# A window-attention and Fourier-mix kernel: constants loaded in another step, start masks and sink halves in other steps and on another engine, transposes in another order

## The chip, the cores and the metric

The kernel runs on one core of one Trainium2 chip. The core has five engines that work side by side, each through its own queue of instructions in order: TensorE (PE, matrix products, with its weight loads shown as PEld), VectorE (DVE), ScalarE (ACT), GpSimd (POOL) and SyncE (SP), which issues loads and stores. POOL can issue loads too, into a queue of its own. Sixteen DMA engines carry out what the queues hold. Engines wait for one another by semaphores.

The metric is device time in microseconds (us) of one launch. The kernel before ran three times: 782.7, 784.17 and 782.69 us, median 782.7 us.

## The reference

```python
B, H, S, D = 4, 8, 768, 64; n_sink, window = 4, 128; d_model = 512
scores = (q @ k^T) / sqrt(D)
keep   = (key < n_sink) | (0 <= query - key < window)
a      = softmax(where(keep, scores, -1e9))
x      = (a @ v), heads side by side          # B x 768 x 512
u      = x + real(fft(fft(x, axis=1), axis=2))
un     = (u - mean(u)) / sqrt(var(u) + 1e-6)
out    = u + relu(un @ w_ch1) @ w_ch2         # 512 -> 2048 -> 512
```

So there are three things in a row: attention with four sink keys and a window of 128 keys, a two-dimensional Fourier transform of which the real part is added, and a feed-forward block. The input `window` is read at run time, so the masks are made on the chip.

## The kernel before

**Attention in steps.** The 24 blocks of 128 queries (4 batches of 6) are taken one after the other, in the batch order 0, 2, 1, 3. Each block g is worked on in four steps s = 4g + k, one for each pair of heads. A step's work is spread over later steps as a software pipeline. `STEP_LAG` says how many steps later each part runs: scores on PE and the merge and masked reduction on DVE in the step itself (`merge`, `soft1`), the exponentials on ACT two steps later (`expo`), the transposes `pt` of the probabilities on PE three later (`trans_p`), ACT's copy `pta` four later, POOL's two selections five later (`newer_p`, `older_p`), the products `xt` with the values seven later (`av`). `BLOCK_AT` gives the same for work done once per block, counted from step 4g: `floor` (POOL adds 1e-9 to the sums), `inverse` (DVE's reciprocal of them, L743), `trans_sink` (PE's transpose `pk` of the sink probabilities), `turn_x` (PE's `x`, which turns the block's result and adds the sink part) and `store_x` (DVE scales by the reciprocal).

**Order within a step.** `SCHEDULE` has two phases, before step 36 and from 36 on, and in each phase a list for every engine and each k: the order in which the engine's pieces are issued in that step. The names "A", "V", "G", "T" in a list stand for events of that engine: one-off pieces that `at(step, engine, fn)` has put there, such as the parts of the Fourier transform on PE ("T"). The scores are issued two steps at a time, ahead of the T list, into two PSUM buffers. Up to step 97 (`CUT`) this hand-made order holds; behind it an automatic scheduler orders what is left.

**Loads.** SP loads a block's queries and keys two blocks ahead (`q`, `ring`, or both in `ld` for a batch's first block), the values `ldv`, and a batch's sink values `vt`. `ring` is a ring of eight key blocks. A score product whose two key blocks wrap around the end of the ring waits for every load into the ring that was issued before it; that is so in step 28 (block 7).

**The start.** ACT turns the sink values into a high half `vs` (`sink_hi`, L682) and DVE writes the low half into the other partitions (`sink_lo`, L686); for the first batch this happens in step `SINK0_AT`. DVE makes the masks: mask 0 ahead of step 0, then `other_masks` in step 4 (L885 to L895: the two `older` masks, which say where the window's older block is to be merged, and the sink columns and window columns of masks 1 to 3), and `last_mask` in step 6.

**Fourier mix.** Its constants `cst` (3348 KB) and `cst_row` (322 KB) are loaded once, by POOL, in `load_constants` (L292 to L296), which also clears `sph` and `zr`. It is called in step 4, ahead of that step's POOL events. As the blocks of a batch are done, DVE and POOL fold them, and PE runs stage 1 in five pieces (za, za, zr, zb, zb), each in one or two parts. After each piece ACT copies a high half (`z_hi`) and DVE forms the low half (`z_lo`) in the step that follows the piece's last part (L487). Stage 1's pieces take turns in PSUM with the transposes; in steps 81 to 97 they have one bank.

**Feed-forward.** High and low halves again, products of 128x512 on PE (`h`, `o`). They begin beside the attention and fill PE alone from about 280 us to the end.

## Time and profile before

| what | before |
|---|---|
| runs | 782.7, 784.17, 782.69 us |
| the profiled execution | 786.08 us |
| its span, first to last instruction | 784.1 us |
| mean granted PE clock | 0.991 |
| busy: PE, DVE, ACT, POOL | 755.7, 453.5, 237.1, 185.1 us |
| bytes moved | 57.67 MB |

The profile page is one execution. Its second part cuts the span into 40 equal slices and gives each engine's busy share in tenths. A row of the timeline has the start, the duration, the engine, the line of the code, what is written and read, a count where equal instructions are put together, and in brackets the idle time of the engine before it and the instruction that ended that. A row of the windows has, for a stretch of the span, the busy time of each engine, then the granted clock of PE, the mean busy share of the sixteen DMA engines and what they moved in GB/s. A row of the waits has the engine and line, what it waited for, the total, how often, and the longest. All stand at the prediction.

### The profile page before, as it was taken

To read this page: it belongs to the slowest core of one execution; us is meant where nothing else is said; L and a number is where in the kernel's file an instruction comes from. 1 tells how busy PE (TensorE), PEld (TensorE's weight loads), DVE (VectorE), ACT (ScalarE), POOL (GpSimd) and SP (SyncE) were. 2 spreads that over 40 slices of the span, in tenths; PEclk is the share of its full clock that TensorE was granted. 3 is DMA by queue.
4 is the path that set the end of the run, shared out by engine and by line. 5 is a ranking of instruction groups with operands and counts; after the bars stand their busy time and mean duration, and the time that the engine had idled before them with its cause. 6 is when DMAs were issued, how large, how long until landed. Compare 5 with 4: busy or idle time off the path is not lost.

```text
span 784.1 us, 11917 instructions
## 1 busy us (share of the span) xinstructions
PE 755.7 (96%) x4379; PEld 616.8 (79%) x4379; DVE 453.5 (58%) x1330; ACT 237.1 (30%) x704; POOL 185.1 (24%) x307
## 2 busy tenths in 40 slices
PE   7999998989998999999999999999999999999996
PEld 5676876867777878899888888888888888888895
DVE  6878587999999489561456424661456424611211
ACT  4887765766523123221111101111111111110110
POOL 2567477477654255100000000000000000000000
PEclk9999999999999899999999999999999999999998
DMA  9863535434215266110100002000200001000100
GB/s 283 268 177 105 151 83 177 127 112 145 86 50 166 92 196 208 66 59 1 54 0 1 1 18 89 1 0 1 81 0 1 2 1 54 1 0 1 54 1 31
DMA packets 41810, 57.67 MB, mean 74 GB/s; under 512 B 2796, under 2 KB 27500, under 8 KB 41360
## 3 DMA queue, kind: packets, MB, share of 16 engines
q1 hardware_dynamic: 41456, 53.07, 21.6%
q0 software_dynamic: 288, 3.76, 1.3%
q8 instruction: 36, 0.59, 0.3%
q14 instruction: 30, 0.25, 0.1%
HBM read 47.37 MB, written 9.45 MB: 72 GB/s over the span
## 4 chain that ended last, share of the span: by engine, by line
PE 80%; DVE 9%; POOL 4%; issue 3%; ACT 2%; DMA 2%; SPq 1%; POOLq 0%; DVEq 0%; ACTq 0%
PE o L1126 33%; PE h L620 33%; PE s L703 3%; PE xt L793 3%; PE pt L755 2%; PE za L395 1%; DVE cv L592 1%; DVE cv L593 1%; DVE sm L721 1%; PE zb L395 1%; ACT pta L762 1%; ACT sm L727 1%; DMA vt<-in_v_sink_dram 1%; POOL ptl L771 1%; DVE s L709 1%
## 5 line engine op out<-in xcount | busy, mean ns | idle before, releaser
L1126 PE MATMUL o<-w,h 128*128 128x512 f32 x876 | 218.6, 397 | 0.0
L1119 DVE SCALAR_TENSOR_TENSOR h<-h,h 128x512 fp32r<-128x512 f32 (+1 forms) x107 | 65.4, 611 | 250.5 <-ACT h L1114 250.3
L1126 PEld LDWEIGHTS o<-w,h 128*128 128x128 f32 x876 | 164.5, 190 | 36.0
L1114 ACT ACTIVATE h<-h 128x512 fp32r<-128x512 f32 (+1 forms) x107 | 57.1, 534 | 368.6 <-PE h L620 362.4
L620 PE MATMUL h<-un_slots,w 128*128 128x512 f32 (+1 forms) x576 | 124.7, 365 | 0.0
L620 PEld LDWEIGHTS h<-un_slots,w 128*128 128x128 f32 x576 | 99.6, 188 | 19.6
L620 PE MATMUL h<-un_last,w 128*128 128x512 f32 (+1 forms) x432 | 89.0, 355 | 0.0
L620 PEld LDWEIGHTS h<-un_last,w 128*128 128x128 f32 x432 | 72.7, 188 | 12.8
L727 ACT ACTIVATE sm<-sm,mx 128x132 f32<-128x132 f32 x192 | 76.0, 400 | 6.0 <-DVE mx L721 6.0
L1150 DVE STREAM_TRANSPOSE unf<-un 32x128 f32<-32x128 f32 x224 | 67.7, 302 | 3.2
L703 PE MATMUL s<-ring,q 64*128 64x260 f32 x320 | 49.9, 418 | 8.9 <-DVE mx L721 5.3
L721 DVE CUSTOM_DVE_ANT_0 sm<-s,mask 128x132 f32<-128x132 f32 x192 | 48.5, 293 | 6.3 <-PE s L701 1.3
L703 PEld LDWEIGHTS s<-ring,q 64*128 64x128 f32 x320 | 27.3, 188 | 21.6 <-issue 8.0
L609 POOL TENSOR_TENSOR w<-cv,w 128x512 fp32r<-128x512 f32 x25 | 34.1, 1366 | 30.5 <-ACT w L608 30.5
L793 PE MATMUL xt<-ptl,ldv 128*64 128x128 f32 x384 | 39.3, 285 | 0.2 <-POOL ptl L771 0.2
L727 ACT ACTIVATION_READ_ACCUMULATOR sm<-sm,mx 128x1 f32 x192 | 36.7, 191 | 0.0
L1126 PE MATMUL o<-w_ring,h 128*128 128x512 f32 x144 | 35.6, 393 | 0.0
L762 ACT COPY pta<-pt 128x512 f32<-128x512 f32 x48 | 28.0, 583 | 24.9 <-PE pt L755 23.5
L709 DVE COPY_PREDICATED s<-older,s 128x256 f32<-128x256 uint8 x80 | 33.7, 421 | 1.6 <-PE s L703 1.6
L771 POOL TENSOR_SCALAR_AFFINE_SELECT ptl<-pta 128x512 f32<-128x512 f32 x48 | 32.5, 678 | 7.3 <-ACT pta L762 7.2
L793 PEld LDWEIGHTS xt<-ptl,ldv 128*64 128x64 f32 x384 | 21.9, 136 | 15.1 <-issue 6.2
L793 PE MATMUL xt<-pta,ldv 128*64 128x128 f32 x320 | 31.7, 274 | 0.3 <-POOL pta L779 0.3
(197 smaller groups left out, 1039.4 us busy)
## 6 DMA issues: line engine op xcount, KB each, us to landing
raw<-in_moe_w_ch_dram SPq DMA_DIRECT2D x32, 512.0 KB, 3.7
ldv<-in_v_dram SPq DMA_DIRECT2D x28, 256.0 KB, 3.3
ring<-in_qk_dram SPq DMA_DIRECT2D x24, 264.0 KB, 4.8
out_dram<-u SPq DMA_DIRECT2D x24, 256.0 KB, 2.1
q<-in_qk_dram SPq DMA_DIRECT2D x20, 256.0 KB, 4.4
cst<-in_dft_dram POOLq DMA_DIRECT2D x1, 3348.0 KB, 12.8
ud<-us SPq DMA_DIRECT2D x12, 256.0 KB, 2.1
u<-ud SPq DMA_DIRECT2D x2, 1024.0 KB, 4.9
```

Of the source, the lines that this page charges most:

```text
L620: T.matmul(ps[:, :tb], a[:, cs], x[:, :, cc, :], start=n == 0, stop=n == 3 * NCC - 1)
L703: T.matmul(ps[:, j, :P + W], st["q", g][rows, hp, :], keys(g, 2 * hp + j), start=True, stop=True)
L709: V.copy_predicated(ps[:, :, P + NS:P + W], older[qi > 2], ps[:, :, 0:P])
L721: V.tensor_tensor_reduce(sm[:, h % 4], ps[:, j, P:P + W], mask[min(qi, 3)], -SCALE, 3.0e38, ALU.add, ALU.min, accum_out=mx[:, 0, h:h + 1])
L727: A.activation(sm[:, h % 4], sm[:, h % 4], AF.Exp, bias=mx[:, 0, h:h + 1], scale=-1.0, accum_out=mx[:, 1, h:h + 1])
L762: A.copy(a, st.pop(("pt", g, hp // 2)))
L771: G.affine_select(lo, a, [[0, 4], [s, P]], compare_op=ALU.is_ge, fill=0.0, base=0, channel_multiplier=-s)
L793: T.matmul(ps[D * j:D * j + D, p, :], st["v", kb(g) - i][:, h, :], a[:, h % 4, :], start=i == 0, stop=i == n - 1)
L1114: A.activation(h[0], ps[:, :tb], AF.Relu)
L1119: V.scalar_tensor_tensor(h[1], ps[:, :tb], 0.0, f32(h[0]), op0=ALU.max, op1=ALU.subtract)
L1126: T.matmul(po[i], a[:, ts_], x, start=f == 0 and n == 0, stop=f == NF - 1 and n == 2)
L1150: V.transpose(unf[32 * q:32 * q + 32, :, r], un[r].rearrange("p (c q j) -> p c q j", c=NCC, q=4)[:, :, q])
```

## The change

Five things change; the arithmetic stays what it was.

1. The first batch's `sink_hi` and `sink_lo` go from step 3 to step 8.
2. `load_constants` is called in step 14 instead of step 4.
3. The two `older` masks are made by POOL right at the start, the plain sink columns of masks 2 and 3 by POOL in step 2, and the rest of `other_masks` by DVE in step 3 instead of 4.
4. `inverse` goes from step 4g + 8 to 4g + 9. From step 36 on, in a block's first step (k = 0), PE's `turn_x` stands ahead of the transposes of the probabilities. (`trans_sink`, which no longer stands in that list, has its turn in k = 1.)
5. `z_lo` of the first and the third piece of stage 1 comes one step later, except in the last batch.

```diff
-SINK0_AT = 3, 3, "V"
+SINK0_AT = 8, 8, "V"
+CONST_AT = 14
 PHASE = 36
...
-    "inverse": 8,
+    "inverse": 9,
...
         "T": [
-            ["av", "trans_p", "trans_sink", "T", "turn_x"],
+            ["av", "turn_x", "trans_p", "T"],
...
                     at(k, "A", lambda kind=kind, mc=mc: z_hi(kind, mc))
-                    at(k, EV_Z, lambda kind=kind, mc=mc: z_lo(kind, mc))
+                    at(k + (not tail and i in (0, 2)), EV_Z, lambda kind=kind, mc=mc: z_lo(kind, mc))
...
                         A.copy(ident_r, ident)
+                        for i, op in enumerate((ALU.is_gt, ALU.is_lt)):
+                            G.tensor_scalar(older[i], dist[:, None, :].broadcast_to([P, 2, P]), 0.0, None, op0=op)
                         parameters()
...
                         def other_masks():
-                            for i, op in enumerate((ALU.is_gt, ALU.is_lt)):
-                                V.tensor_scalar(older[i], dist[:, None, :].broadcast_to([P, 2, P]), 0.0, None, op0=op)
                             V.tensor_scalar_add(sdist, sdist, float(P))
                             V.tensor_scalar(ts, sdist, win_ap, BIG, op0=ALU.is_lt, op1=ALU.mult)
                             V.tensor_tensor(mask[1][:, :NS], ts, nosink, op=ALU.add)
-                            for i in (2, 3):
-                                V.tensor_copy(mask[i][:, :NS], nosink)
...
-                        at(4, "V", other_masks)
+                        def plain_sinks():
+                            for i in (2, 3):
+                                G.tensor_copy(mask[i][:, :NS], nosink)
+
+                        at(2, "G", plain_sinks)
+                        at(3, "V", other_masks)
...
-                                        if (s, op) == (4, "G"):
+                                        if (s, op) == (CONST_AT, "G"):
                                             load_constants()
```

Before, POOL's queue at the start goes from the two parts of the identity to the sink probabilities `sk` of block 0, and then to the constants:

```order
11 masks.py:199 AFFINE_SELECT ident<-ident 128x128
12 L738 CAST sk_215<-sm_0_172 128x2x16
13 L739 TENSOR_TENSOR sk_215<-sm_0_172,sk_215 128x2x16
14 L294 MEMSET sph 128x384
15 L294 MEMSET zr 128x386
16 L295 DMA cst<-in_dft_dram 128x6696
17 L296 DMA cst_row<-in_dft_row_dram 128x644
18 L738 CAST sk_215<-sm_2_195 128x2x16
```

Now the masks stand in the first of these places, and the constants between the two selections `ptl` and `pta` of step 14:

```order
11 masks.py:199 AFFINE_SELECT ident<-ident 128x128
12 L866 TENSOR_SCALAR older_121<-scratch 128x256
13 L866 TENSOR_SCALAR older_122<-scratch 128x256
14 L945 COPY mask_125<-nosink 128x4
15 L945 COPY mask_126<-nosink 128x4
16 L741 CAST sk_222<-sm_0_174 128x2x16
...
36 L774 AFFINE_SELECT ptl_1_471<-pta_1_443 128x512
37 L296 MEMSET sph 128x384
38 L296 MEMSET zr 128x386
39 L297 DMA cst<-in_dft_dram 128x6696
40 L298 DMA cst_row<-in_dft_row_dram 128x644
41 L782 AFFINE_SELECT pta_1_443<-pta_1_443 128x512
```

The block of four rows has moved behind twenty-two other rows of POOL.

On DVE, before, this stands between the last reduction of block 0 (step 3) and the first merge of block 1 (step 4, the row with `s_1_0`):

```order
31 L686 TENSOR_TENSOR vs_0_208<-vt_0_141,vs_0_208 64x512
32 L885 TENSOR_SCALAR older0_121<-scratch_110 128x256
33 L885 TENSOR_SCALAR older1_122<-scratch_110 128x256
34 L887 TENSOR_SCALAR sf_119<-sf_119 128x4
35 L888 TENSOR_SCALAR ts_127<-sf_119,eff_71 128x4
36 L889 TENSOR_TENSOR mask1_124<-ts_127,nosink_120 128x4
37 L891 COPY mask2_125<-nosink_120 128x4
38 L891 COPY mask3_126<-nosink_120 128x4
39 L893 SCALAR_TENSOR_TENSOR scratch_110<-scratch_110 128x128
40 L895 TENSOR_SCALAR mask1_124<-scratch_110,eff_71 128x128
41 L895 TENSOR_SCALAR mask2_125<-scratch_110,eff_71 128x128
42 L709 COPY_PREDICATED s_1_0_225<-older0_121,s_1_0_225 128x2x128
```

Now six rows stand there, and the low half of the sink values comes in step 8, ahead of the first merge of block 2:

```order
31 L890 TENSOR_SCALAR sf_119<-sf_119 128x4
32 L891 TENSOR_SCALAR ts_127<-sf_119,eff_71 128x4
33 L892 TENSOR_TENSOR mask1_124<-ts_127,nosink_120 128x4
34 L894 SCALAR_TENSOR_TENSOR scratch_110<-scratch_110 128x128
35 L896 TENSOR_SCALAR mask1_124<-scratch_110,eff_71 128x128
36 L896 TENSOR_SCALAR mask2_125<-scratch_110,eff_71 128x128
37 L712 COPY_PREDICATED s_1_0_232<-older0_121,s_1_0_232 128x2x128
...
65 L261 CAST outside_72<-bad_320 128x1
66 L689 TENSOR_TENSOR vs_0_317<-vt_0_143,vs_0_317 64x512
67 L712 COPY_PREDICATED s_2_0_309<-older0_121,s_2_0_309 128x2x128
```

The subtraction, the two `older` masks and the two copies have left the place; nothing else has come into it.

On PE, in step 36 (the first of phase two, where no part of the Fourier transform stands), the order before is:

```order
126 L793 MATMUL xt_1046<-pta_1_960,ldv_803 64x128 x2
127 L755 MATMUL pt_1_1055<-ident,sm_0_936 128x128 x4
128 L805 MATMUL x_1060<-ident,xs_1006 128x128 x4
129 L807 MATMUL x_1060<-vs_722,skt_980 128x512
130 L811 MATMUL pk_1083<-ident_r,sk_917 128x128
131 L703 MATMUL s_2_1085<-ring,q_816 128x260 x2
```

And now:

```order
126 L796 MATMUL xt_1045<-pta_1_959,ldv_803 64x128 x2
127 L808 MATMUL x_1054<-ident,xs_1006 128x128 x4
128 L810 MATMUL x_1054<-vs_722,skt_980 128x512
129 L758 MATMUL pt_1_1060<-ident,sm_0_935 128x128 x4
130 L814 MATMUL pk_1083<-ident_r,sk_917 128x128
131 L706 MATMUL s_2_1085<-ring,q_816 128x260 x2
```

`x` and `pt` have changed places, and `pk` follows `pt` directly; the two share a PSUM bank. SP's order of loads and stores is the same before and after.

## The prediction

> **What bounds the kernel now.** I read the page first: busy times, the 40 slices, then the windows of the first 60 us.

> ```profile
> span 784.1 us, 11917 instructions
> PE 755.7 (96%) x4379; PEld 616.8 (79%) x4379; DVE 453.5 (58%) x1330; ACT 237.1 (30%) x704; POOL 185.1 (24%) x307
> PE   7999998989998999999999999999999999999996
> ...
> DMA  9863535434215266110100002000200001000100
> 30.00:40.00 10.00, 9.94 (x99) 7.51 (x99) 8.66 (x45) 8.20 (x33) 5.48 (x15) 1.00 0.72 210
> ```

> PE works 96% of the span. Only 784.1 − 755.7 = 28.4 us of it are idle, nearly all in the first third; from slice 15 (280 us) on PE is full, so a shift made before that is kept to the end. The change touches no matmul count that matters. It is worth what it does to PE's waits, and there are few: 0.06 us in 30 to 40 us. What may grow is a wait that doesn't exist yet. In a window's row the last columns are PE's granted clock, the DMA share (0.72 here, while PE is full) and GB/s.

> **The start: earlier masks, a later sink half.** Removed from the front of DVE's step 3 and 4 are the subtraction into `vs` and the two `older`.

> ```profile
> 4.21 5.88 DMA vt<-in_v_sink_dram
> 10.11 0.62 ACT L682 CAST vs<-vt 128x512 fp32r<-128x512 f32 x1 [3.48 <-DMA vt<-in_v_sink_dram]
> 10.77 0.69 DVE L686 TENSOR_TENSOR vs<-vt,vs 64x512 fp32r<-64x512 f32 x1 [2.44 <-ACT vs L682]
> 11.49 0.51 DVE L885 TENSOR_SCALAR older<-scratch 128x256 uint8<-128x256 f32 x2
> 11.59 0.26 POOL L738 CAST sk<-sm 128x32 fp32r<-128x32 f32 x1 [9.79 <-ACT sm L727]
> 12.85 0.78 POOL L295 DMA_DIRECT2D cst<-in_dft_dram  x1
> 13.90 0.42 DVE L709 COPY_PREDICATED s<-older,s 128x256 f32<-128x256 uint8 x1
> ...
> 11.85 0.60 PE L872 MATMUL warm<-ident 128*128 128x128 f32 x4
> 15.02 2.13 PE L703 MATMUL s<-ring,q 64*128 64x260 f32 x8 [2.57 <-DVE mx L721]
> 15.00:19.00 4.00, 3.98 (x18) 2.27 (x20) 3.55 (x22) 1.34 (x6) 0.56 (x2) 0.57 0.86 351
> ```

> The load of `vt` lands at 10.09; ACT's cast waits 3.48 us for it, DVE's subtraction 2.44 us for ACT, and behind that stand `older`, the masks and the first merge at 13.90. PE's scores of steps 6 and 7 need the buffer which that merge's step frees: 2.57 us idle. Now DVE goes from 8.33 (10.77 − 2.44) straight to the masks that are left: from the end of the two `older` (11.49 + 0.51) to 13.90 are 1.9 us, less the two copies that POOL takes, so they end near 10.1. The merge is then ready 3.8 us earlier, and PE can start step 6 right behind its warm-up, at 11.85 + 0.60 = 12.45: **the 2.57 us go**. The clock was granted at 0.57 over 15 to 19 us, behind this idle time: 0.43 × 4 = 1.72 us of PE time, which goes too if the pause does. Together 4.29 us; about 0.5 of the 0.69 us of the subtraction come back in step 8, where it now stands ahead of a merge. I take **−3.8 us**, with ends −1.9 (2.57 less 0.69, the clock falling anyhow) and −4.3. POOL does the two `older` in time that it spent waiting (9.79 us before 11.59).

> [...] Here an idle time of 2.57 us was already followed by 0.57. [...]

> **The constants: ten steps later.** In the old place they move in a time when PE has loads in hand. In the new one they meet loads that are needed at once.

> ```profile
> cst<-in_dft_dram POOLq DMA_DIRECT2D x1, 3348.0 KB, 12.8
> ldv<-in_v_dram SPq DMA_DIRECT2D x2, 256.0 KB, 10.2
> ...
> q0 software_dynamic: 80, 2.14, 96.5%
> q1 hardware_dynamic: 86, 0.09, 4.4%
> 16.00:17.00 1.00, 1.00 (x5) 0.42 (x4) 0.85 (x3) 0.00 (x0) 0.00 (x0) 0.50 1.06 429
> ...
> 30.29 0.24 POOL L747 TENSOR_SCALAR mx<-mx 128x8 f32<-128x8 f32 x1
> 32.25 0.21 POOL L738 CAST sk<-sm 128x32 fp32r<-128x32 f32 x1 [1.72 <-ACT sm L727]
> ...
> 36.17 0.33 SPq L672 DMA_DIRECT2D ldv<-in_v_dram  x1
> 43.77 0.62 SPq L665 DMA_DIRECT2D ring<-in_qk_dram  x1
> 43.90 0.33 PE L793 MATMUL xt<-ptl,ldv 128*64 128x128 f32 x2
> 49.06 1.15 PE L703 MATMUL s<-ring,q 64*128 64x260 f32 x8
> ring<-in_qk_dram SPq DMA_DIRECT2D x24, 264.0 KB, 4.8
> 31.00:49.00 18.00, 17.54 (x184) 13.14 (x180) 13.87 (x69) 15.06 (x61) 10.41 (x26) 1.00 0.80 228
> ```

> The two queue rows and the `ldv` row above them (10.2 us to landing) are those of 14 to 20 us. POOL's queue (q0) moved 80 packets of 27 KB and took 96.5% of the engines' time, SP's queue (q1) 86 small ones: the engines take one of each in turn, so while `cst` flows the loads of keys, queries and values all but stand still. 3348 + 322 KB at 429 GB/s are 8.8 us. In step 14 POOL stands near 30 us on this trace's clock (30.29 is the `floor` of that step, behind which the issue now stands less one select), so `cst` flows from about 32 to 41 us.

> What SP loads then: from 31 to 49 us the 16 engines were busy 0.80 × 18 = 14.4 us. With 8.8 us more they need 23.2 us: the last of that work lands at 31 + 23.2 = 54.2 instead of about 48.6 (the `ring` load issued at 43.77, +4.8). Step 28's first scores at 49.06 wrap around the key ring and wait for just this load, with 0.5 us in hand. **So PE waits 54.2 − 49.06 = 5.1 us** by then, part of it already at 43.90 for the values issued at 36.17. If a long backlog moves bytes faster than this sparse one, the bound is lower: 228 GB/s × 18 us = 4.10 MB at the 336 GB/s of the busiest stretch without `cst` (row below) are 12.2 us, the end is 31 + 12.2 + 8.8 = 52.0, and the wait 2.9 us. I take 4.5, nearer the first since the packets stay small. This wait doesn't depend on the start's gain: needs, issues and `cst` all move forward by the same 3.8 us.

> ```profile
> 24.00:26.00 2.00, 2.00 (x24) 1.32 (x24) 1.85 (x12) 1.98 (x9) 0.73 (x5) 1.00 1.10 336
> 254.84 1.66 PE L422 MATMUL a<-cst,za 128*128 128x258 f32 x6 [2.62 <-DVE zb L410]
> 254.00:262.00 8.00, 7.16 (x22) 6.08 (x23) 1.47 (x3) 1.73 (x4) 1.28 (x1) 0.57 0.24 80
> ```

> Pauses of this length cost clock as well: behind the other long one (2.62 us, before 254.84) the clock was 0.57 over 8 us, 3.4 us of PE time; the first cost 1.72. Two pauses of 2 to 3 us could cost 3.4; none if they come in short pieces. I take +1.0, since DVE and POOL bound much of 50 to 63 us. The issues (0.78 us for `cst`, with the row's and two memsets about 2 us) also stand ahead of a select of step 14; POOL waits 1.72 us soon after (before 32.25), so I count **+0.2** of it, between nothing and 2.

> **x ahead of pt.** From step 36 on, in a block's first step, `x` and `pt` change places. Where a Fourier part follows, `pk` finds its bank free as before. In steps 36 and 60 none does, and `pk` now follows `pt` at once, and needs the copy of `pt` out of the PSUM bank that they share.

> ```profile
> 64.97 0.66 PE L755 MATMUL pt<-ident,sm 128*128 128x128 f32 x4
> ...
> 66.30 0.28 PE L811 MATMUL pk<-ident_r,sk 128*128 128x128 f32 x1
> L762 ACT COPY pta<-pt 128x512 f32<-128x512 f32 x48 | 28.0, 583 | 24.9 <-PE pt L755 23.5
> ```

> Before, `x` covered this copy. Now its 0.58 us and about 0.1 of hand-over lie open, less what PE's queue runs past the end of `pt`: two times 0.5, **+1.0** (0 to 1.4).

> **Reciprocal and low halves.**

> ```profile
> DVE zr L407 <- ACT zr L400: 3.4, 2, 1.7
> DVE za L410 <- ACT za L402: 3.1, 4, 1.6
> DVE mx L743 <- POOL mx L747: 2.3, 3, 1.1
> L709 DVE COPY_PREDICATED s<-older,s 128x256 f32<-128x256 uint8 x80 | 33.7, 421 | 1.6 <-PE s L703 1.6
> L721 DVE CUSTOM_DVE_ANT_0 sm<-s,mask 128x132 f32<-128x132 f32 x192 | 48.5, 293 | 6.3 <-PE s L701 1.3
> ```

> DVE waited 2.3 us for `floor` at the reciprocal (3 times) and 6.5 us for `z_hi` at the low halves (6 times). Most of it lay beside PE's full stretches. The reciprocal: **−0.6** (−2.3 to 0). In batches 0 and 1 the low halves gain and cost nothing, since PE is full there. In batch 2 (steps 88 to 96) they share one PSUM bank with the next Fourier part: its first matmul now waits for a half that stands behind a merge and two reductions, 0.42 + 2 × 0.29 = 1.0 us; **+0.7** with ends −1 and +2. Behind step 97 the scheduler writes the order anew; I see no reason for a sign there: 0, with 1.5 to both sides.

> **The sum** is −3.8 + 4.5 + 1.0 + 0.2 + 1.0 − 0.6 + 0.7 = **+3.0 us**. On the profiled execution that gives 786.1 + 3.0 = 789.1 (span 784.1, 2 us around it); this one lies 3.4 us above the median of the runs shown. I carry the difference to that median: 782.7 + 3.0 = **785.7 us**.

> **Rivals.** *The constants fit in (faster).* The point that decides is whether the values issued at 36.17 and the ring load issued at 43.77 still land before 43.90 and 49.06. It needs the 3.6 us in which the engines were free (18 − 14.4), and 5 us more from better packing. For it speaks that loads from 14 to 20 us came late too (`ldv`, 10.2) and PE hardly waited; against it, that their users were far off, and that 0.5 us is all the slack of step 28. Then the 4.5 and 1.0 go: 3.0 − 5.5 = −2.5, that is 780.2, and to 778 with the better ends (reciprocal −2.3).

> [...]

> *Nothing in sum.* With the lower bound of the wait, 2.9, and no loss of clock the sum is 3.0 − 1.6 − 1.0 = +0.4: 783.1. That the masks give nothing, since the pause moves to another load of the start, is its counterpart above: −1.9 instead of −3.8 with all waits gives +4.9, 787.6.

> **How the numbers follow.** Waits for loads larger than the start's gain: 0.48 (785.7, own range 784.4 to 790). In sum nothing: 0.18. Constants fit in: 0.34 (778 to 781). 0.2% (1.6 us) is about what a measurement of this kernel can tell from no change, and the three cases are those of slower, same and faster. The range that leaves out 2 in 10 goes from 778.3 to 789.5.

> **What would show it.** Right at the start: the merge near 10, step 6's scores near 12.4 at full clock, step 12's 3 to 4 us before 23.86. Right at the constants: landing of `cst` near 38, loads of 8 us and more between 27 and 45 us, and PE idle with an SP load as releaser before step 28's scores. Wrong: step 28's scores at or before 46 us. Then the sum falls to the rival's. At steps 36 and 60 a wait of `pk` for ACT's `pta` of about 0.6 us; in batch 2 a wait of `za` or `zr` for DVE.

## The result and the profile after

| | before | after |
|---|---|---|
| median of the runs beside each other | 783.43 us (782.69 to 784.49, 4 runs) | 797.09 us (795.47 to 798.52, 4 runs) |
| ratio, 95% interval | 1 | 1.0173 (1.0146 to 1.0200) |
| the profiled execution, its span | 786.08, 784.1 us | 798.52, 796.8 us |
| PE idle in the span | 28.4 us | 39.4 us |

The change costs 13.6 us (11.4 to 15.7 by the interval). The prediction had the sign and +3.0 us, that is 785.7 us; the measured 797.09 us lies above its range (778.3 to 789.5). First the page of the changed kernel: the span, the busy times, PE in 40 slices.

```profile
span 796.8 us, 11919 instructions
...
PE 757.4 (95%) x4379; PEld 619.0 (78%) x4379; DVE 451.3 (57%) x1326; ACT 237.1 (30%) x704; POOL 186.5 (23%) x311
...
PE   8978998988898999999999999999999999999996
```

PE does the same work (757.4 us beside 755.7) and stands still 11 us longer, 10.1 of them before 280 us (31.8 beside 21.7). Where, is read from one instruction that each block has once, `pk`. Its start in the changed kernel less its start before, by the two timelines of PE:

| `pk` of block | 0 | 1 | 3 | 4 | 5 | 10 | 13 | 16 | 19 | 21 | 23 | end of the span |
|---|---|---|---|---|---|---|---|---|---|---|---|---|
| before, us | 21.4 | 27.6 | 40.4 | 46.6 | 52.6 | 93.3 | 118.3 | 148.4 | 176.1 | 195.3 | 212.0 | 784.1 |
| after − before, us | −1.3 | −0.1 | +0.3 | +2.5 | +7.4 | +7.5 | +9.1 | +10.3 | +11.7 | +12.9 | +16.1 | +12.7 |

Three things are seen. The start won nothing. Between blocks 3 and 5 some 7 us are lost, where the constants now flow. And from block 10 to 23 another 9 us go bit by bit, of which the tail gives 3 back, 1.7 of it in clock (before, the clock of 0.57 from 254 to 262 us cost 3.4 us of PE time; now 0.79 from 240 to 248 us costs 1.7). The middle loss in the changed kernel, first in two windows (busy times of PE, PEld, DVE, ACT, POOL, then clock, DMA share, GB/s):

```profile
40.00:50.00 10.00, 7.47 (x78) 5.51 (x76) 4.50 (x23) 7.17 (x28) 4.32 (x11) 1.00 1.04 323
50.00:60.00 10.00, 6.74 (x56) 5.05 (x54) 4.42 (x23) 4.22 (x16) 5.54 (x10) 0.83 0.39 110
```

Then in the timeline of PE, the two rows that waited for a load:

```profile
46.70 0.44 PE L796 MATMUL xt<-ptl,ldv 128*64 128x128 f32 x4 [2.42 <-DMA ldv<-in_v_dram]
...
54.85 1.51 PE L706 MATMUL s<-ring,q 64*128 64x260 f32 x8 [3.20 <-DMA ring<-in_qk_dram]
```

And in the queue rows of its DMA view from 36 to 42 us (packets, MB, share of the engines):

```profile
q0 software_dynamic: 130, 2.24, 89.6%
q1 hardware_dynamic: 132, 0.07, 5.8%
```

Both waits stand at the instructions the prediction had named, for the loads it had named, 5.62 us together. In this stretch the engines took about as many records of one queue as of the other (130 and 132; 80 and 79 from 36 to 41.5 us), and SP's loads, whose records are small (0.07 MB in 132), hardly moved. `cst` landed 13.7 us after its issue at 30.02, that is at 43.7, and not near 38. Behind the second pause (3.20 us) the clock was lower: 0.83 over 50 to 60 us is 1.7 us of PE time. Behind the first (2.42 us) it stayed at 1.00 over 40 to 50 us.

The start, in the timeline of PE before:

```profile
5.80 1.10 PE L872 MATMUL warm<-ident 128*128 128x128 f32 x8
...
7.48 1.53 PE L872 MATMUL warm<-ident 128*128 128x128 f32 x12
```

and after:

```profile
6.18 1.97 PE L877 MATMUL warm<-ident 128*128 128x128 f32 x8
...
9.26 2.42 PE L877 MATMUL warm<-ident 128*128 128x128 f32 x12
...
14.58 1.15 PE L706 MATMUL s<-ring,q 64*128 64x260 f32 x8
```

The pause before step 6 is gone, as predicted. But the same warm-up products took 1.97 and 2.42 us instead of 1.10 and 1.53: PE ran them fast only some 5.5 us later in this execution, and came to step 6 at 14.58, not at 12.4. (This rise is read from the products alone: 0.24 us each while slow, 0.13 when fast. By this an estimate of the rise is 5.5 us before and 11 us after. The column of the granted clock shows 1.00 in both up to 14 us.)

### The profile page after: what moved, and what is told of

Same layout as the page of the kernel before. It is cut to its first block, busy times and chain, and to the rows that moved or that the text cites. A ratio compares the mean times of both kernels' runs of the same rounds, so it can differ in the third digit from the quotient of the medians.

```text
span 796.8 us, 11919 instructions
## 1 busy us (share of the span) xinstructions
PE 757.4 (95%) x4379; PEld 619.0 (78%) x4379; DVE 451.3 (57%) x1326; ACT 237.1 (30%) x704; POOL 186.5 (23%) x311
## 3 DMA queue, kind: packets, MB, share of 16 engines
q1 hardware_dynamic: 41456, 53.07, 21.4%
## 4 chain that ended last, share of the span: by engine, by line
PE 77%; DVE 9%; POOL 5%; issue 3%; DMA 3%; ACT 2%; SPq 0%; DVEq 0%; POOLq 0%; ACTq 0%
PE o L1132 32%; PE h L623 31%; PE xt L796 3%; PE s L706 3%; DMA ldv<-in_v_dram 2%; PE pt L758 1%; PE za L397 1%; DVE sm L724 1%; POOL ptl L774 1%; DVE cv L595 1%; POOL pta L782 1%; ACT sm L730 1%; ACT pta L765 1%; PE zb L397 1%; DVE s L712 1%
## 5 line engine op out<-in xcount | busy, mean ns | idle before, releaser
L623 PEld LDWEIGHTS h<-un_last,w 128*128 128x128 f32 x432 | 72.8, 188 | 12.7
L724 DVE CUSTOM_DVE_ANT_0 sm<-s,mask 128x132 f32<-128x132 f32 x192 | 48.5, 293 | 9.1 <-PE s L704 3.3
L712 DVE COPY_PREDICATED s<-older,s 128x256 f32<-128x256 uint8 x80 | 33.8, 422 | 10.3 <-PE s L706 10.2
## 6 DMA issues: line engine op xcount, KB each, us to landing
ldv<-in_v_dram SPq DMA_DIRECT2D x28, 256.0 KB, 3.5
ring<-in_qk_dram SPq DMA_DIRECT2D x24, 264.0 KB, 4.2
out_dram<-u SPq DMA_DIRECT2D x24, 256.0 KB, 2.1
q<-in_qk_dram SPq DMA_DIRECT2D x20, 256.0 KB, 4.2
cst<-in_dft_dram POOLq DMA_DIRECT2D x1, 3348.0 KB, 13.7
ud<-us SPq DMA_DIRECT2D x12, 256.0 KB, 2.0
```

What stands on the lines that cost most here:

```text
L623: T.matmul(ps[:, :tb], a[:, cs], x[:, :, cc, :], start=n == 0, stop=n == 3 * NCC - 1)
L712: V.copy_predicated(ps[:, :, P + NS:P + W], older[qi > 2], ps[:, :, 0:P])
L724: V.tensor_tensor_reduce(sm[:, h % 4], ps[:, j, P:P + W], mask[min(qi, 3)], -SCALE, 3.0e38, ALU.add, ALU.min, accum_out=mx[:, 0, h:h + 1])
```

## The experiments

Each is the kernel before with the edit shown, unless it says otherwise; each was timed beside the kernel before on the same chip. Differences in us are the ratio's, of 784 us.

**The constants alone (e1).**

```diff
-                                        if (s, op) == (4, "G"):
+                                        if (s, op) == (14, "G"):
```

> The kernel before with the constants in step 14 and nothing else changed. Theory A (the constants meet the loads of keys and values): PE waits for a value load near 44 us and for the ring load before step 28's scores, 5 to 6 us together, with about 2 us of half clock behind it, and the time rises by 6 to 8 us, to about 790.5. Rival B (the loss of the changed kernel is made behind 66 us, by the changed order of transposes and low halves): the waits are there but are made good, and the time rises by under 3 us, to at most 786.

788.41 us beside 784.02, ratio 1.0069 (1.0050 to 1.0088): +5.4 us (3.9 to 6.9). In its timeline of PE, and then in two windows:

```profile
45.09 0.44 PE L793 MATMUL xt<-ptl,ldv 128*64 128x128 f32 x4 [1.97 <-DMA ldv<-in_v_dram]
...
52.93 1.15 PE L703 MATMUL s<-ring,q 64*128 64x260 f32 x8 [1.62 <-DMA ring<-in_qk_dram]
```

```profile
44.00:48.00 4.00, 2.91 (x26) 2.58 (x26) 0.00 (x1) 2.21 (x9) 1.69 (x4) 0.81 1.16 325
48.00:52.00 4.00, 3.31 (x30) 2.45 (x28) 3.48 (x12) 2.54 (x10) 2.27 (x5) 0.76 0.88 234
```

The waits are 3.59 us and the clock costs (0.19 + 0.24) × 4 = 1.7 us, in one stretch from about 46.5 to 49.5 us; behind the second pause it was 1.00 (52 to 56 us). Together 5.3 us. None of that was made good later: `pk`, 1.5 us early at block 0 (a gain that no theory had), is 3.9 us late at block 5 and 3.8 at block 23. So this profile shows a net 3.8 up to block 23, the lower end of what the times show. Rival B falls; theory A holds at its lower end and a little below.

How the second wait came about is read from the chain of work that ended last (start, duration, what):

```profile
40.00 6.79 DMA x0d<-scratch
...
46.86 0.36 SPq L347
...
48.32 4.38 DMA ring<-in_qk_dram
52.69 0.24 issue
52.93 1.15 PE s L703 x8
```

The ring load landed 4.4 us after its issue, no later than before (4.8). But it was issued at 48.32 instead of 43.77, since SP's queue stood: a small store ahead of it (`x0d`, 8 KB), itself behind a load that took 3.58 us to issue, needed 6.8 us to land (3.9 before), and the load behind that store waited for it. In the changed kernel the ring load was issued at 50.95 and landed in 3.7 us; there the chain runs from the late values (10.1 us to landing) through `xt`, which frees their buffer, to SP's next loads.

**The start's two edits alone (e2)**, parts 1 and 3 of the change.

```diff
-SINK0_AT = 3, 3, "V"
+SINK0_AT = 8, 8, "V"
...
+                            G.tensor_scalar(older[i], dist[:, None, :].broadcast_to([P, 2, P]), 0.0, None, op0=op)
...
-                        at(4, "V", other_masks)
+                        at(2, "G", plain_sinks)
+                        at(3, "V", other_masks)
```

> The kernel before with the start's two edits alone: older masks and plain sink columns on POOL, the other masks in step 3, both halves of the sink values in step 8. The prediction's theory: the scores of step 12 come 3.8 us earlier and the time falls to about 779.6. Rival A2 (read from the changed kernel's trace): the pause before step 6 goes, but the low half in step 8 waits for ACT behind its exponentials and takes 1.6 us back, so step 12 gains about 2 us at full clock and nothing where the first warm-up runs at the low clock; the time is 781 to 783.5. Rival C (POOL's mask work at the start itself delays the clock's rise): the eight warm-up products near 6 us take about 2 us instead of 1.1 again in the profile.

785.79 us, ratio 1.0028 (1.0015 to 1.0042): **+2.2 us, slower**, above what either theory gave. The warm-up was slow here too (1.97 us), which fits C; some unchanged starts show the same, so C isn't settled by this run (see below).

**The changed kernel with the constants back in step 4 (e3).**

```diff
-CONST_AT = 14
+CONST_AT = 4
```

> The changed kernel with the constants back in step 4. Theory A: the two waits for loads and the half clock behind them go, and the time falls by 6 to 8 us, to about 790; what is left above the kernel before, some 6 us, is made behind 66 us. Rival B: it falls by under 3 us, to 794 or more. A third way: with the start earlier, the constants in step 4 hold up the loads of steps 8 to 16 and PE waits there 1 to 3 us, so the time is 791 to 793.

792.42 us, 1.0110 (1.0094 to 1.0125): 4.9 us below the changed kernel by the two ratios, between the theories, and in the range of the third way. PE did wait at the start, 1.36 us for the ring load before step 12.

**x ahead of pt alone (e4).**

```diff
-            ["av", "trans_p", "trans_sink", "T", "turn_x"],
+            ["av", "turn_x", "trans_p", "T"],
```

> The kernel before with the order of x and pt (k = 0, from step 36 on) alone. The prediction's size: +1.0 us (0 to 1.4), 784.4. Theory A as read from the changed kernel's trace, where pk waits three times 0.5 to 0.7 us for ACT's copy and x once 1.4 us for a low half of stage 1: +2 to +4 us, about 786. Rival B2 (the order costs nothing, the low halves do): within 0.5 us of the kernel before.

791.80 us, 1.0098 (1.0080 to 1.0116): **+7.7 us**, the costliest part by far, and twice what I had expected even with the changed kernel's trace at hand. Four rows of PE's timeline before:

```profile
99.97 0.29 PE L422 MATMUL a<-cst_row,zr 128*128 128x258 f32 x1
100.09 0.60 PE L805 MATMUL x<-ident,xs 128*128 128x128 f32 x4
100.45 0.47 PE L807 MATMUL x<-vs,skt 128*128 128x512 f32 x1
100.76 0.95 PE L443 MATMUL b<-cst,zb 128*128 128x258 f32 x6
```

And of this run, where the second and third (`a`, then `b`) answer to the first and the last of those:

```profile
66.54 0.28 PE L811 MATMUL pk<-ident_r,sk 128*128 128x128 f32 x1 [0.68 <-ACT pta L762]
...
100.41 0.28 PE L422 MATMUL a<-cst_row,zr 128*128 128x258 f32 x1
101.16 1.00 PE L443 MATMUL b<-cst,zb 128*128 128x258 f32 x6 [0.47 <-ACT asb L431]
...
147.80 0.66 PE L805 MATMUL x<-ident,xs 128*128 128x128 f32 x4 [0.74 <-DVE zb L410]
...
186.60 0.66 PE L805 MATMUL x<-ident,xs 128*128 128x128 f32 x4 [1.03 <-DVE un_slots L554]
...
214.05 0.44 PE L793 MATMUL xt<-ptl,ldv 128*64 128x128 f32 x4 [1.53 <-POOL ptl L771]
```

Before, `x` stood between the products `a` and `b` of the Fourier part, and its 0.7 us covered ACT's copy `asb` of `a` (0.37 us), for which `b` waits. Now `b` stands behind `a` directly. That is one kind of wait; `pk` behind `pt` is the second. In the third `x` itself comes too soon: its PSUM bank still holds a piece of stage 1, or a transpose of the layer norm, that DVE has not read. In the fourth, `pt` stands behind such an `x`, and POOL's selection comes late and with it `xt` (1.53 us). From 60 to 290 us PE idles 20.2 us in this profile and 15.3 in that of before, so 4.9 of the 7.7 us are seen as waits; where the rest lies isn't shown.

**The low halves alone (e5); the reciprocal alone (e6).**

```diff
-                    at(k, EV_Z, lambda kind=kind, mc=mc: z_lo(kind, mc))
+                    at(k + (not tail and i in (0, 2)), EV_Z, lambda kind=kind, mc=mc: z_lo(kind, mc))
```

> The kernel before with the two low halves of stage 1 one step later (not in the last batch) alone. The three runs of single parts so far add up to +13.6 us of the changed kernel's +13.7, so theory A3 (the parts add) leaves nothing for this one and the reciprocal: within 1 us of the kernel before. The prediction's size was +0.7 (784.7 beside 784.0). Rival (parts don't add, and x ahead of pt loses to the low halves in the changed kernel what it lost to others alone): +2 us or more.

784.99 us, 1.0014 (0.9997 to 1.0031): +1.1 us, not told apart from nothing. In its profile the waits are where they were expected, in batch 2 (waits of PE from 180 to 215 us; before, 0.7 for `zb` and none for `za`):

```profile
PE zb L395 <- DVE zb L410: 1.8, 1, 1.8
PE za L395 <- DVE za L410: 1.0, 1, 1.0
```

The reciprocal:

```diff
-    "inverse": 8,
+    "inverse": 9,
```

> The kernel before with the reciprocal one step later alone. Theory A3 (the parts add): within 1 us. The prediction's size: -0.6 us (-2.3 to 0), 783.4 beside 784.0.

784.43 us, 1.0006 (0.9988 to 1.0024): no difference that can be told.

**The masks alone (e7), and the sink halves alone (e8)**: the two edits of the start, of which the diff is above, taken apart. The first has all of it but `SINK0_AT`, the second that line alone.

> The kernel before with the masks' edit alone (older masks and plain columns on POOL, the rest in step 3); the sink halves stay in step 3. Theory D (at the start, PE's warm-up work bounds the scores of step 6 when the clock rises late, and DVE's masks when it rises early; the loss of the start's run lies in step 8): step 6's scores follow the warm-up without a wait and the time is 0 to 1.5 us below the kernel before, 782.5 to 784. Rival: the masks' edit itself costs, for POOL's two older masks take 1.7 us beside DVE and slow it: 785 or more.

782.63 us, 0.9974 (0.9958 to 0.9989): **−2.0 us, faster** (0.9 to 3.3), a little beyond theory D's 0 to 1.5, and the rival is out. Step 6 didn't wait; but the clock rose late in this profile, and then unchanged starts don't wait there either.

> The kernel before with the sink halves in step 8 alone, the masks as before. Theory D: the low half waits for ACT's cast, which stands behind step 6's four exponentials, and holds up the merge of step 8 by 1.5 us, while the start gains only where step 6 waited for DVE: 784.5 to 786.5. Rival (the prediction's): the vt load no longer holds up step 4's merge, so 2 us are won and 0.5 given back: 782.5.

786.55 us, 1.0028 (1.0011 to 1.0045): +2.2 us. Theory D's number, but the profile shows another reason than D's. In it the clock rose early (rows of its timeline, POOL and PE):

```profile
8.65 0.78 POOL L295 DMA_DIRECT2D cst<-in_dft_dram  x1
...
11.95 1.15 PE L703 MATMUL s<-ring,q 64*128 64x260 f32 x8
...
24.93 1.41 PE L703 MATMUL s<-ring,q 64*128 64x260 f32 x8 [3.99 <-DMA ring<-in_qk_dram]
```

Step 6 starts at 11.95 without a pause, the prediction's 12.45 and better, and `pk` of block 0 is 3.7 us early. Then step 12 waits 3.99 us for a ring load. ACT, which no longer stands waiting for the sink values, does its exponentials sooner, POOL reaches step 4 sooner, and the constants are issued at 8.65 instead of 12.85, among the start's loads.

**Half of the new order: x ahead of the Fourier part, but behind pt (e9).**

```diff
-            ["av", "trans_p", "trans_sink", "T", "turn_x"],
+            ["av", "trans_p", "turn_x", "T"],
```

> The kernel before with x ahead of the Fourier part but behind pt (list av, trans_p, turn_x, T), so that one half of the new order is left. x ahead of everything cost 7.7 us. Theory X1 (pt comes too late, and with it ACT's copy, POOL's selections, xt and pk): pk's two waits of 0.68 us and the late xt go, and 0 to 2.5 us are left, at most 786.8. Theory X2 (x comes too early: its PSUM bank is still held by a Fourier part or a layer-norm transpose, and PE stands still in front of it): 790 or more.

788.56 us beside 783.58, 1.0071 (1.0052 to 1.0089): +5.6 us, between X1 and X2 and nearer to X2. `pk` no longer waits and `xt` is not late; what is left are waits around the Fourier parts (waits of PE, 62 to 262 us; before, `b` waited 1.0 us and the other two not at all):

```profile
PE za L395 <- ACT asb L431: 2.5, 1, 2.5
PE b L443 <- ACT asb L431: 2.5, 4, 1.0
...
PE dc L422 <- DVE zb L410: 1.8, 1, 1.8
```

`x` itself still waits for its bank, 1.4 us in all, and PE idles as long from 60 to 290 us as in the run before (20.1 us). So some 5.6 of the 7.7 us come from `x` going ahead of the Fourier part; the rest, by the intervals anything from 0 to 4 us, comes from `pt` standing behind `x`.

**x ahead of pt in steps 36 to 71 alone (e10).**

```diff
-                                for op in SCHEDULE[s >= PHASE][e][k]:
+                                for op in (["av", "turn_x", "trans_p", "T"] if (e, k) == ("T", 0) and 36 <= s < 72 else SCHEDULE[s >= PHASE][e][k]):
```

> The kernel before with x ahead of pt in steps 36 to 71 alone. By the milestones of the run with the whole order (pk of block 15 is 1.7 us later than at block 5, the end 8 to 9 us) this costs +1 to +2 us, 785.3 to 786.3; the rest lies in steps 72 to 96 and behind, where DVE and POOL have no time in hand. Rival: the early steps carry most, for PE is full there: +4 us or more.

786.50 us, 1.0041 (1.0025 to 1.0056): +3.2 us (2.0 to 4.4), above theory and below rival. The loss is spread over both halves.

**Masks, with the constants in step 8 (e11)**: the masks' edit, and this.

```diff
-                                        if (s, op) == (4, "G"):
+                                        if (s, op) == (8, "G"):
```

> The kernel before with the masks' edit and the constants in step 8, sink halves in step 3. Theory: the start's loads are through by then and the values and keys that meet the constants have 7 us and more in hand, so nothing is lost and up to 1 us won against the masks alone: 781 to 782.5. Rival: the values issued between 18 and 23 us arrive too late and PE waits 2 us or more: 784 or more.

782.66 us beside 783.58, 0.9988 (0.9975 to 1.0000): −0.9 us. In its profile no load makes PE wait between 6 and 50 us, so the rival is out. Nothing shows a gain on the masks alone.

**The changed kernel with the old order of pt and x (e12).**

```diff
-            ["av", "turn_x", "trans_p", "T"],
+            ["av", "trans_p", "trans_sink", "T", "turn_x"],
```

> The changed kernel with the old order of pt and x. Theory (the parts add): 7 to 8 us of its loss go, 789 to 790. Rival (the order costs less beside the low halves and the late constants, which leave PE waiting anyway): 792 or more.

791.51 us, 1.0106 (1.0086 to 1.0127): 5.2 us less than the changed kernel by the two ratios, between theory and rival.

**The start with the constants out of its way**: both start edits with the constants in step 8 (e13); the same with `SINK0_AT = 5, 9, "V"` (e14); and both start edits with the constants in step 14 (e15).

> Both start edits (masks, sink halves in step 8) with the constants in step 8. Theory M (the constants of step 4 met the start's ring load: 1.4 us of waiting for it in the start's own run, 4.0 in the sink's): the wait for the ring load before step 12 goes, and the time falls from +2.2 to about +0.5 against the kernel before, 784. Theory P (the low half ahead of step 8's merge is the price): it stays at +1.5 or more, 785.5.

784.71 us beside 785.02, 0.9992 (0.9976 to 1.0009): −0.6 us, so 2.8 us better than with the constants in step 4, and PE waits for no load in the first 60 us. Theory M holds, P falls.

> The masks' edit, the constants in step 8, the sink's high half in step 5 and its low half in step 9, where DVE's list has it behind merge and reductions. Theory P: without the low half in the way this is 1.5 us better than the run with step 8 and at least as good as the masks alone, 781 to 782.5. Theory L (the clock's late rise bounds the start): no better than masks and constants in step 8, 782.5 to 783.5.

782.86 us, 0.9985 (0.9968 to 1.0002): −1.2 us, not told apart from the run before it. The low half's place is worth nothing that shows.

> Both start edits with the constants in step 14, and none of the other parts: the part of the change that the prediction summed to +1.9 (-3.8 + 4.5 + 1.0 + 0.2). From the single runs: constants +5.4 and start +2.2 less the 1.4 to 2 us by which the start's loss came from the constants in step 4, so +5.5 to +6, 789 to 789.8. Rival (the start's gain shows once the constants are out of its way): +2 to +3, 786.

789.74 us, 1.0064 (1.0046 to 1.0083): +5.0 us (3.6 to 6.5), beside +5.4 for the constants alone. The rival is out: with the constants of the change in place, the start's edits win about 0.4 us, by intervals that overlap widely.

**When the clock rises** could be read off all 17 profiles, since the first warm-up products are the same in each. In 6 of them (among these the profile of before on which the prediction rests) the eight products near 6 us took about 1.1 us, in 11 about 2. Start of `pk` of block 1, by kernel and by rise:

| start | early rise | late rise |
|---|---|---|
| unchanged | 27.58, 27.41, 27.32 | 26.99, 27.01, 26.75 |
| unchanged, constants in step 14 | 26.04 | |
| sink halves alone | 30.00 | |
| both edits, constants in step 4 | | 28.32, 27.71 |
| both edits, constants in step 8 | 24.92 | |
| both edits, constants in step 14 | | 26.48, 26.58; the changed kernel 27.44 |
| masks alone | | 25.95 |
| masks, constants in step 8 (the second with `SINK0_AT = 5, 9`) | | 25.81, 25.83 |

With the late rise there is no pause to win: PE is held up by its own slow warm-up and comes to step 6 between 13.6 and 14.6 us without a wait, in unchanged starts as well. With the early rise the unchanged starts pause for 2.57, 2.23 and 2.11 us there, and PE is slow behind each: in the profile of before the clock was 0.57 over 15 to 19 us (1.7 us lost), in e6 and e10 the eight scores after the next `pt` took 2.22 us, where 1.15 is usual. With the constants in step 14 (e1) the pause is 1.38 us and the four scores behind it take 0.71 us, as they do at a clock of 1.00 (16 to 20 us in the changed kernel). Both edits together with the constants out of the way then win 2.5 us at block 1; but 1.4 of these come with the constants alone (26.04), so the start's own part is about 1.1, from one execution each. With the late rise edits and constants together win 0.2 to 0.5.

Of the 8 profiles without the masks' edit 5 had the early rise, of the 9 with it only one. So rival C, that POOL's mask work delays the rise, stays open: the counts speak for it, but they are few, and the first rows of PE are the same in all.

## Why the prediction was wrong

The sign was right, and the waits of the likeliest case came. The size was not: +3.0 against +13.6, also outside that case's own range (784.4 to 790). Term by term, with what the run of the part alone measured:

| term of the sum | predicted | measured |
|---|---|---|
| start: masks, sink halves | −3.8 | −0.4 (with the constants in step 14, 5.0 − 5.4; by the two intervals about −2.5 to +1.7) |
| constants: waits 4.5, clock 1.0, select 0.2 | +5.7 | +5.4 (3.9 to 6.9) |
| x ahead of pt | +1.0 | +7.7 (6.3 to 9.1); beside the other parts 5.2 |
| reciprocal | −0.6 | +0.5 (−0.9 to 1.9) |
| low halves | +0.7 | +1.1 (−0.2 to 2.4) |
| sum | +3.0 | +14.3 of the parts, +13.6 of the whole |

**The step that failed most is "x ahead of pt".** It said "Where a Fourier part follows, `pk` finds its bank free as before" and counted the two places where none does. That is true of `pk`, and its two waits of 0.68 us came as described. But `pk` was the wrong thing to ask about alone. What `x` itself had covered was left out: in the timeline of before it stands inside the Fourier parts, between a product and the one that needs a copy of it. And I did not ask what holds the bank that `x` writes, at the time to which it was moved. Run e9 puts about 5.6 of the 7.7 us on these two omissions.

**The start was mis-sized.** The pause and its price (2.57 + 1.72 us) were read from one execution, in which the clock rose early; with the late rise (8 of the 9 profiles with the masks' edit, 3 of the 8 without) there was no such pause. Where the clock was early the pause went as predicted, and `pk` of block 0 came 3.7 us sooner in e8. Also missed was that freeing ACT brings the constants forward (issued at 8.65 us in e8, 12.85 before), if they stay in step 4. In the change they don't, so this is a loss of e2, e3 and e8, and not of the changed kernel.

**The constants were right as a sum, but in part by luck.** Two waits at the two named instructions and a lower clock behind one of them came: 3.59 us for 4.5, and 1.7 for 1.0. In the changed kernel itself they are 5.62 and 1.7; why the waits are longer there than in e1 isn't settled, and each is one execution. The path to the second wait was another than predicted. The prediction let the ring load be issued in time and land late, at 54.2, behind 8.8 us of work for the sixteen engines. In both kernels that load landed sooner after its issue than before (4.4 and 3.7 us for 4.8), but its issue came 4.6 and 7.2 us late, because SP's queue waited behind earlier loads and stores. And the 1.5 us that were won ahead of block 0 when the constants left step 4 were not in the sum. Two readings were off as well: the stretch of 24 to 26 us, taken as one without `cst`, still holds 84 records of POOL's queue; and the 86 records of SP's queue beside POOL's 80 from 14 to 20 us all lie before 15.5 us. From 15.5 to 20 us the view shows POOL's queue alone, though SP issued four loads from 17.18 us on:

```profile
q0 software_dynamic: 64, 1.71, 92.4%
```

The rival "constants fit in" is refuted: PE waited 5.62 us in the changed kernel for the two loads it named. There the records of the two queues stand one for one from 36 to 41.5 us, 80 and 79. That the engines always take one of each in turn, as the prediction has it, isn't shown: from 15.5 to 20 us of the profile of before it was 64 and none.

In e1 the clock fell behind the pause of 1.97 us (0.81 over 44 to 48 us, 0.76 over 48 to 52) and not behind that of 1.62 us (1.00 over 52 to 56); in the changed kernel it stayed behind the pause of 2.42 us (1.00 over 40 to 50) and fell behind that of 3.20 us (0.83 over 50 to 60). In these four the shortest pause with a fall, 1.97 us, is shorter than the longest without one, 2.42 us; what decides is not shown.

The parts add up only roughly. The changed kernel without the new order loses more than its parts (e12, +8.3 us, beside 5.0 + 0.5 + 1.1), and with the constants in step 4 less (e3, +8.6, beside 2.2 + 7.7 + 0.5 + 1.1); both gaps are no wider than the intervals together allow.

Of all these kernels the masks alone beat both: 0.9974 (0.9958 to 0.9989) of the time before.

## What to carry to other kernels

When an instruction is moved in an engine's order, ask three things: what waits for it, what waited behind it, and what it had been covering where it stood. The third is invisible as long as it works, and is read from the neighbours of the instruction in the timeline, not from any wait. And a pause that is to be removed should be looked for in several executions before its price goes into a sum; a large load belongs where the queue has no load with a user near (here step 8: in e11 no wait of PE for a load from 6 to 50 us, where step 14 brought 3.59 us in e1), and a part of the program that runs sooner takes its loads with it (the constants' issue by 4.2 us in e8). When a load comes late, look whether it was issued late or landed late.

## What was not expected of the hardware

What a pause costs in clock differed as well. The same wait of `a` for `zb` near 255 us, 2.62 us in the profile of before, was followed there by 3.4 us of lost PE time (0.57 over 254 to 262 us). The next twelve products `o` took 5.01 us there, 3.47 us in e1 (wait 2.60 us) and 2.90 us in e6 (2.53 us).

And one of SP's ring loads took 3.58 us to issue in e1 while the constants flowed, where 0.62 us was usual before:

```profile
36.32 3.58 SPq L665 DMA_DIRECT2D ring<-in_qk_dram  x1
```

In the changed kernel it took 3.98 us. The store `x0d` that stands next in SP's queue was issued at 40.00 us in e1 and 41.53 in the changed kernel, for 37.87 before. Why the issue took so long is not shown.
